# Attention and phase-mixing MLP on one core: theta weights in two loads, and the q/k preparation of two pairs moved to the boundary before theta

## The chip, the core and the metric

The kernel runs on one core of a Trainium2 chip. A core has five engines with a queue of instructions each: TensorE (PE, matrix products and transposes), VectorE (DVE), ScalarE (ACT, table functions and copies), GpSimd (POOL) and SyncE (SP). Each works through its own queue in order and waits on semaphores that the others, or a finished transfer, count up. Transfers between memory and the core run on 16 DMA engines; here POOL issues all loads but two, and SP issues the stores of the output and the transposing transfers.

The metric is the device time of one execution in microseconds (us). The kernel before has a median of 172.26 us in three runs (171.69 to 172.28).

## The reference

```python
# attention, for 4 batches, 8 heads, 768 positions, head size 64
scores = q @ k.T / sqrt(64) - slope[h] * dist        # per head
keep   = (first 8 positions) | (0 <= i - j < 96)
a      = softmax(where(keep, scores, -1e9));  x = a @ v     # x: (4, 768, 512)
# phase-mixing MLP
theta = x @ w_theta                                  # 512 x 512
y = w_tok_r @ (x * cos(theta)) + w_tok_i @ (x * sin(theta)) # 768 x 768 each
u = x + y
out = u + relu(u @ w_ch)                             # 512 x 512
```

Only a band of the scores counts: for each block of 128 keys the queries of the same and of the next block, and the first 8 positions for everybody.

## The kernel before, in words

Heads go in four pairs of two (128 rows for two heads of 64); positions go in six blocks of 128. The stages of a batch, with the names of the functions and the lines of the profile:

- *Loads.* `load_w` (L160) issues on POOL's queue the token weights in six pieces, the theta weights in one transfer of 512 KB (L168), q and k of batch 1, and the channel weights; behind it come v of batch 1 and q and k of batch 2. All these loads convert float32 to bfloat16 on the way. v of batch 2 and the first half of the heads of q and k of batch 3 are issued during batch 0's mixing. `load_behind` (L496) lets POOL copy one element of xT of batch 1 (the "gate", L497) and issues the other half of batch 3's q and k, and its v, behind that copy. The queue's transfers take turns on eight completion semaphores, so each waits until the eighth transfer before it has landed.
- *Preparation of q and k, `prep`* (L249) for one batch and pair: DVE copies q and k of the pair into `qkn` (L246, two copies a pair, for two pairs at once at the start), PE transposes six blocks each of q and k (L261), DVE brings q's transposes to `qT` (L265) and ACT k's to `kT` (L267), and DVE makes `kG` from `kT` (L235, L237). Batch 3's q and k are transposed by SP's transfers instead (`prep_dma`).
- *Scores and values.* `score_mms` (L319) fills a bank group `pb`; there are two such groups, and values use them too. ACT takes the exponential (L329), DVE multiplies by a table of the bias (L338, L341). `values` (L381) multiplies by v and by `vG` (v with the global rows, DVE L359, L360); DVE divides by the row sums into `x_sb` (L386, L388).
- *xT.* `xtrans` turns `x_sb` of a pair into `xT`. For pairs 0, 1 and 2 of batches 1 and 2 it is a transposing transfer on SP's queue (L392); for pair 3 it is six PE transposes (L399) and an ACT copy (L400).
- *Theta.* `theta` (L422) multiplies `xT` by the theta weights, four blocks of 128 inner elements for each of the six position blocks, in the order block 0, 1, 2 (3 last) so that pair 2's `xT` is first needed by the third product. ACT takes cosine and sine (L432), DVE multiplies them with x into `zri` (L436).
- *Mixing.* `mix` (L447) multiplies the transposed token weights with `zri`, DVE adds x into `u` (L452). `utrans` turns `u` (PE L465 and an ACT copy L466, or an SP transfer L461). `chan` (L475) multiplies by the channel weights, DVE adds relu and `u` (L480), SP stores the result (L482).

While batch b is mixed, the attention of batch b+1 runs: `weave` puts the steps of both into one order by weights given by hand. Before the change, the preparation of pairs 0 and 1 of batch 2 is a part of that weave for b = 0 (list `ahead`, L652), that of pairs 2 and 3 is in the weave for b = 1. At the boundary between two batches stands a list `order` (L654): the first remaining `chan` group of batch b-1, four pieces of theta of batch b, another `chan` step, the rest of theta, the rest of `chan`.

Up to `manual.close()` (L642) each engine's order is as written. Behind it a scheduler sets each engine's order from the order of issue and from what each instruction needs, so the position of an instruction on its engine is read from the built program. `behind(...)` keeps a preparation's instructions behind the last one named there on the same engine.

Of the kernel before, what the change touches and what calls it, by code (L numbers as in the profile page):

```python
# [16 lines left out]
def kernel(  # L17
# [13 lines left out]
    nc = tc.nc  # L31
    B, H, S, D = q.shape
    T = 128
    NT = S // T
    DM = H * D
    NC = DM // T
    NP = H // 2
# [18 lines left out]
    def ps_small(shape, dtype):  # L56
        return small.tile(shape, dtype, name="ps", tag="ps")
# [5 lines left out]
    def alloc_qk(b):  # L63
        loads[b] = [ld.tile([T, 2, H, NT, D], BF, name="qk"), None]

    def alloc_v(b):
        vn = loads[b][1] = ld.tile([T, H, NT, D + 1], BF, name="vn")
        nc.vector.memset(vn[:, :, :, D:D + 1], 1.0)

    def load_qk(b, h0, n, which=(0, 1)):  # L70
        qk = loads[b][0]
        for i_ in which:
            nc.gpsimd.dma_start(
                out=qk[:, i_, h0:h0 + n].rearrange("p h t d -> p h (t d)"),
                in_=(q, k)[i_][b, h0:h0 + n].rearrange("h (p t) d -> p h (t d)", p=T))
# [10 lines left out]
    def load_v(b, h0, n):  # L86
        vn = loads[b][1]
        nc.gpsimd.dma_start(out=vn[:, h0:h0 + n, :, 0:D].rearrange("p h t d -> p (h t) d"),  # L88
                            in_=v[b, h0:h0 + n].rearrange("h (t p) d -> p (h t) d", p=T))
# [8 lines left out]
    for i_, eng in ((1, nc.sync), (0, nc.scalar)):  # L98
        eng.dma_start(out=qk32[:, i_].rearrange("p h t d -> p h (t d)"),
                      in_=(q, k)[i_][0, 0:2].rearrange("h (p t) d -> p h (t d)", p=T))  # L100
# [54 lines left out]
    w_theta_bf = const.tile([T, NC, DM], BF)  # L155
# [2 lines left out]
    w_tokT = [const.tile([T, NT, S], BF, name=f"w_tokT_{wi}") for wi in range(2)]  # L158

    def load_w():  # L160
        for tt in range(0, NT, 2):
            for wi, src in enumerate((moe_w_tok_r, moe_w_tok_i)):
                w2 = moe.tile([T, 2, S], BF, name="w_nat", bufs=6)
                nc.gpsimd.dma_start(
                    out=w2, in_=src[tt * T:(tt + 2) * T, :].rearrange("(a p) s -> p a s", p=T))
                w_nat[wi, tt], w_nat[wi, tt + 1] = w2[:, 0], w2[:, 1]
            if tt == 0:
                nc.gpsimd.dma_start(out=w_theta_bf, in_=moe_w_theta.rearrange("(c p) n -> p c n", p=T))  # L168
            if tt == NT - 4:
                load_all_qk(1)  # L170
        nc.gpsimd.dma_start(out=w_ch_bf, in_=moe_w_ch.rearrange("(c p) n -> p c n", p=T))

    def trans_w(tt, copy=nc.vector.tensor_copy, wide=False, copy0=nc.vector.tensor_copy):
        pb = big.tile([T, 2, 2 * 512], BF, name="pbw", tag="pb") if wide else None
        tiles = [pb[:, wi, 0:S].rearrange("p (t n) -> p t n", t=NT) if wide else ps_small([T, NT, T], BF)
                 for wi in range(2)]
        for wi, ps in enumerate(tiles):
            for st in range(NT):
                nc.tensor.transpose(ps[:, st, :], w_nat[wi, tt][:, st * T:(st + 1) * T], ident)
            if not wide:  # L180
                (copy if wi else copy0)(out=w_tokT[wi][:, :, tt * T:(tt + 1) * T], in_=ps)
        for wi, ps in enumerate(tiles if wide else ()):
            (copy if wi else copy0)(out=w_tokT[wi][:, :, tt * T:(tt + 1) * T], in_=ps)  # L183
# [17 lines left out]
    def behind(eng):  # L201

        return tc.issue_after(anchor[eng]) if eng in anchor else nullcontext()
# [25 lines left out]
    def kglob(b, p, t0=0, t1=NT - 2, copy=nc.vector.tensor_copy):  # L229
        kT = qkT[(b, p)][1]  # L230
        if t0 == 0:
            qkT[(b, p)][2] = att.tile([T, NT - 2, T], BF, name="kG", bufs=6)
        kG = qkT[(b, p)][2][:, t0:t1]
        with behind("zri" if p else "dve") if b == B - 1 else nullcontext():
            copy(  # L235
                out=kG, in_=kT[:, (t0 + 1) * T:(t1 + 1) * T].rearrange("p (t n) -> p t n", t=t1 - t0))
            copy(out=kG[:, :, 0:NG], in_=kT[:, None, 0:NG].to_broadcast([T, t1 - t0, NG]))  # L237
# [3 lines left out]
    def prep_copy(b, p):  # L241
        qk = loads[b][0]
        qkn = qkns[b, p] = att.tile([T, NT, 2, 2, D], BF, name="qkn", bufs=2)
        with behind("dve"):
            for i_ in range(2):
                nc.vector.tensor_copy(  # L246
                    out=qkn[:, :, i_].rearrange("p t h d -> p h t d"), in_=qk[:, i_, 2 * p:2 * p + 2])

    def prep(b, p):  # L249
        if p == 0 or (b, p) == (2, NP // 2):  # L250
            prep_copy(b, p)
        if p + 1 < NP and (b, p) != (2, NP // 2 - 1):
            prep_copy(b, p + 1)
        qkn = qkns[b, p]
        qT = att.tile([T, S], BF, name="qT", bufs=6)
        kT = att.tile([T, S], BF, name="kT", bufs=6)
        for i_, dst in ((0, qT), (1, kT)):
            ps = ps_small([T, NT, T], BF)
            with behind("pe"):
                for t_ in range(NT):  # L260
                    nc.tensor.transpose(ps[:, t_, :], qkn[:, t_, i_].rearrange("p h d -> p (h d)"), ident)  # L261
            dst = dst.rearrange("p (n t) -> p n t", t=NT)
            src = ps.rearrange("p t n -> p n t")
            if i_ == 0:
                nc.vector.tensor_copy(out=dst, in_=src)  # L265
            else:
                nc.scalar.copy(out=dst, in_=src)  # L267

        qkT[(b, p)] = [qT, kT, None]
        kglob(b, p)  # L270

    def prep_dma(b, p):
        qk = loads[b][0]
        qkT[(b, p)] = [None, None, None]
        for i_ in (1, 0):
            to = qkT[(b, p)][i_] = att.tile([T, S], BF, name=("qT", "kT")[i_], bufs=6)
            with behind("sp"):
                nc.sync.dma_start_transpose(
                    out=to.rearrange("p (t s) -> p t s", t=NT),
                    in_=qk[:, i_, 2 * p:2 * p + 2].rearrange("p h t d -> p (h t d)"))  # L280
# [204 lines left out]
    def load_all_qk(b):  # L485
        alloc_qk(b)
        load_qk(b, 0, 8)

    def load_all_v(b):
        alloc_v(b)  # L490
        load_v(b, 0, 8)
# [39 lines left out]
    def weave(main, side, s0=0.0, s1=1.0):  # L531
# [11 lines left out]
        while i_ < len(side):  # L543
            side[i_][1]()
            i_ += 1

    load_w()
    load_all_v(1)
    load_all_qk(2)
    alloc_x(0)  # L550
    dve, act = nc.vector.tensor_copy, nc.scalar.copy
    warm(6)
# [53 lines left out]
    p = NP - 1  # L606
# [39 lines left out]
    rest = []  # L646
    for b in range(B):
        nxt = b + 1 if b + 1 < B else None
        lag = 3
        th = [lambda c=c, j=j: theta(b, c, j) for c in range(NT // 2) for j in range(2)]  # L650
        pre = [lambda p=p: prep(1, p) for p in range(NP)] if b == 0 else []
        ahead = [[lambda p=p: prep(2, p) for p in range(NP // 2)], [lambda p=p: prep_dma(3, p) for p in range(1)],  # L652
                 [], []][b]
        order = rest[:1] + th[:4] + rest[1:2] + th[4:] + rest[2:] if b else []  # L654
        if b == 2:
            order[:0] = [lambda p=p: prep_dma(3, p) for p in range(1, NP)]
        if b == 1:
            order.insert(0, lambda: load_behind(3, xT_sb[1][0:1, NC - 1, 0:1]))
        for f in order:
            f()  # L660
        main = []
        for tt in range(0 if b else 2, NT):
            for g in range(NT // 2):
                if (b, tt) != (B - 1, NT - 1):
                    main.append((2048, lambda tt=tt, g=g: mix(b, tt, g)))
                if b == 0 and g == 1 and 4 <= tt + 2 < NT:
                    main.append((1536, lambda tt=tt: trans_w(tt + 2)))
                if tt >= lag and g == 0 and (b, tt) != (B - 1, NT - 1):
                    main.append((2048, lambda tt=tt: chan(b, tt - lag)))
                if b == 0 and g == 1:  # L670
                    main.append((512, lambda tt=tt: utrans(b, tt - 1)))
                if (b, tt, g) == (0, 2, 0):
                    main.append((512, lambda: utrans(0, 0)))
            if b and (b, tt) != (B - 1, NT - 1):
                main.append((0, lambda tt=tt: utrans(b, tt)))
        side = [(1536, f) for f in pre]
        if b == 0:
            side[:0] = [(0, lambda: load_all_v(2))]
            side.append((0, lambda: (alloc_qk(3), load_qk_tokens(3, 0, H // 2))))
        side += attention_steps(nxt, ahead) if nxt else []  # L680
        weave(main, side, 0.1 if b == 0 else 0.0, 0.9)
        rest = [lambda tt=tt, b=b: chan(b, tt) for tt in range(NT - lag, NT)]
        if b == 0:
            rest.insert(1, lambda b=b: utrans(b, NT - 1))
# [44 lines left out]
```

## Time and profile before

| What | us |
|---|---|
| median of three runs | 172.26 |
| span of the profiled execution (first to last instruction) | 170.0 |
| median less that span (start and end around it) | 2.3 |
| PE busy / DVE busy / ACT busy / POOL busy | 158.1 / 125.9 / 102.1 / 37.6 |
| theta weights: issued, landed | 9.98, 24.48 |
| v of batch 2: issued, landed | 39.86, 62.4 |
| first product of theta of batch 0 / third of batch 1 | 24.56 / 70.73 |

Of the profiled execution only the span is given, not a time of its own; the third line is therefore a difference between two executions. The granted clock of PE is 1.00 in all stretches. PE's busy share is high all through (its matmuls are pipelined and a group's busy time overlaps the next), so the page's busy row says little; what counts is which engine a stretch waits for. The chain of work that ended last gives that, the timeline of each engine gives the order of the instructions and their idle times, and the transfers' view gives the time from issue to landing.

### The profile page before, as it was taken

What the parts mean: (1) busy time and instruction counts of PE and PEld (TensorE: products, weight loads), DVE (VectorE), ACT (ScalarE), POOL (GpSimd) and SP (SyncE); (2) the same over time, 40 slices, a digit from 0 to 9 for tenths busy, and PEclk for the clock granted to TensorE, in tenths of its full rate; (3) what the DMA queues carried; (4) which work ended last, traced back from release to release, by engine and by line L of the source; (5) the groups of instructions that cost most, each with busy time, mean ns of one, the idle gap of its engine ahead of it and who ended that gap; (6) DMA issues with size and microseconds to landing.
All of it is one profiled execution on the core that took longest, in us unless ns stands there. A gap on an engine that the chain in (4) does not pass through costs nothing.

```text
span 170.0 us, 3773 instructions
## 1 busy us (share of the span) xinstructions
PE 158.1 (93%) x1544; PEld 85.4 (50%) x1566; DVE 125.9 (74%) x267; ACT 102.1 (60%) x131; POOL 37.6 (22%) x45
## 2 busy tenths in 40 slices
PE   7679999999989899799999999999999999999991
PEld 2346765657645555345555464444554644444440
DVE  6748877699989999957998787788776847614432
ACT  4698898995596585399954561899257309400010
POOL 8976319005262110696000000000000000000000
PEclk9999999999999999999999999999999999999999
DMA  4999999999999999999996879688135472233335
GB/s 147 205 171 179 210 207 205 203 209 180 152 203 189 188 153 182 127 163 149 184 112 57 165 167 130 132 152 241 35 77 139 113 169 80 109 61 93 93 93 185
DMA packets 73488, 25.53 MB, mean 150 GB/s; under 512 B 61568, under 2 KB 70528, under 8 KB 73472
## 3 DMA queue, kind: packets, MB, share of 16 engines
q0 software_dynamic: 45680, 12.45, 77.1%
q1 hardware_dynamic: 27376, 12.33, 32.9%
q10 hardware_dynamic: 416, 0.52, 0.9%
q8 instruction: 12, 0.20, 0.5%
q14 instruction: 4, 0.03, 0.0%
HBM read 25.69 MB, written 6.29 MB: 188 GB/s over the span
## 4 chain that ended last, share of the span: by engine, by line
PE 56%; DMA 19%; DVE 16%; ACT 6%; issue 2%; DVEq 0%
PE ps L447 26%; DMA vn<-in_v_dram 14%; PE ps L475 9%; PE pb L422 6%; PE pb L319 4%; PE pb L381 3%; PE ps L422 3%; DMA xT<-x_sb 3%; DMA qk<-in_k_dram 3%; DVE x_sb L388 3%; DVE e L338 2%; ACT e L329 2%; PE ps L215 1%; ACT cs L432 1%; DVE e L341 1%
## 5 line engine op out<-in xcount | busy, mean ns | idle before, releaser
L447 PE MATMUL ps<-zri,w_tokT 128*128 128x512 bf16 x272 | 67.5, 380 | 1.1 <-issue 0.3
L329 ACT ACTIVATE e<-pb 128x1024 bf16<-128x1024 f32 (+1 forms) x48 | 43.4, 954 | 17.4 <-PE pb L319 17.0
L447 PEld LDWEIGHTS <-w_tokT 128*128 128x128 bf16 x288 | 25.9, 98 | 27.8 <-DVE w_tokT L183 0.6
L452 DVE TENSOR_TENSOR u<-x_sb,ps 128x512 bf16<-128x512 bf16 x24 | 16.3, 680 | 11.7 <-PE ps L447 11.6
L475 PE MATMUL ps<-w_ch_bf,uT 128*128 128x512 bf16 (+1 forms) x96 | 24.1, 371 | 0.2
L436 DVE TENSOR_TENSOR zri<-x_sb,cs 128x1024 bf16<-128x1024 bf16 (+1 forms) x30 | 16.6, 581 | 6.3 <-ACT cs L432 6.1
L480 DVE SCALAR_TENSOR_TENSOR o_sb<-ps,u 128x512 f32<-128x512 f32 (+1 forms) x25 | 16.4, 663 | 4.1 <-PE ps L475 4.1
L319 PE MATMUL pb<-qT,kT 64*128 64x128 bf16 x224 | 15.4, 219 | 2.2 <-DVE qT L226 1.2
L338 DVE TENSOR_TENSOR e<-e,etab 128x1024 bf16<-128x1024 bf16 (+1 forms) x24 | 14.8, 618 | 3.1 <-ACT e L329 3.0
L432 ACT ACTIVATE cs<-pb,halfpi 128x1024 bf16<-128x1024 f32 x8 | 8.9, 1116 | 12.5 <-PE pb L422 12.4
L422 PE MATMUL pb<-w_theta_bf,xT 128*128 128x512 bf16 x62 | 15.0, 379 | 1.1 <-DMA xT<-x_sb 0.9
L319 PEld LDWEIGHTS <-kT 64*128 64x128 bf16 x224 | 8.9, 94 | 13.2 <-issue 11.3
L466 ACT COPY uT<-ps 128x512 bf16<-128x512 bf16 x7 | 4.2, 594 | 18.3 <-PE ps L465 18.1
L381 PEld LDWEIGHTS <-e 128*128 128x128 bf16 x352 | 13.0, 97 | 4.3 <-issue 1.6
L422 PEld LDWEIGHTS <-xT 128*128 128x128 bf16 x96 | 9.1, 98 | 11.8 <-DMA xT<-x_sb 1.9
L475 PEld LDWEIGHTS <-uT 128*128 128x128 bf16 x100 | 9.1, 98 | 9.6 <-ACT uT L466 0.8
L88 POOL DMA_DIRECT2D vn<-in_v_dram x5 | 9.6, 1915 | 12.7 <-DVE qkn L246 10.4
L319 PE MATMUL pb<-qT,kG 64*128 64x128 bf16 x128 | 11.5, 216 | 0.3 <-DVE kG L237 0.2
L388 DVE TENSOR_TENSOR x_sb<-pb,rec 128x768 bf16<-128x768 f32 x12 | 11.4, 953 | 0.3
L381 PE MATMUL pb<-vn,e 128*128 128x65 bf16 x168 | 9.9, 193 | 0.7 <-DVE x_sb L388 0.3
L341 DVE TENSOR_TENSOR e<-e,etab 128x1024 bf16<-128x1024 bf16 x12 | 8.2, 687 | 2.4 <-ACT e L329 2.4
L267 ACT COPY kT<-ps 128x768 bf16<-128x768 bf16 x8 | 6.4, 798 | 4.6 <-PE ps L261 4.4
(81 smaller groups left out, 209.4 us busy)
## 6 DMA issues: line engine op xcount, KB each, us to landing
out_dram<-o_sb SPq DMA_DIRECT2D x23, 256.0 KB, 2.3
vn<-in_v_dram POOLq DMA_DIRECT2D x3, 768.0 KB, 22.5
qk<-in_q_dram POOLq DMA_DIRECT2D x2, 768.0 KB, 21.1
qk<-in_k_dram POOLq DMA_DIRECT2D x2, 768.0 KB, 24.2
w_nat<-in_moe_w_tok_r_dram POOLq DMA_DIRECT2D x3, 384.0 KB, 15.7
w_nat<-in_moe_w_tok_i_dram POOLq DMA_DIRECT2D x3, 384.0 KB, 15.2
vn<-in_v_dram POOLq DMA_DIRECT2D x2, 384.0 KB, 10.2
qk<-in_q_dram POOLq DMA_DIRECT2D x8, 96.0 KB, 8.6
```

The source lines that it names most:

```text
L319: nc.tensor.matmul(pb[:, hh, o:o + T], lhsT=lhsT, rhs=qT[R, (own, nxt)[part]], start=bool(b), stop=bool(b) or (jt == NT - 1 or (j == 1 and ...
L329: ins = nc.scalar.activation(e_c, pb[:, :, 0:n], AF.Exp, scale=scale).ins
L338: nc.vector.tensor_mul(e_c, e_c, tab[:, :, s0:s0 + n // T].rearrange("p a s n -> p a (s n)"))
L381: nc.tensor.matmul(po4[:, head - h0, it - i0], lhsT=l_, rhs=r_, start=(i_ == 0), stop=(i_ == len(mms) - 1))
L388: nc.vector.tensor_mul(xv, po4[:, :, :, 0:D], rec.to_broadcast([T, n, nt, D]))
L422: nc.tensor.matmul(pb[j_] if last else pb[:, j_, :], lhsT=xT[:, dc, st(j_)], rhs=w_theta_bf[:, dc, :], start=(dc == 0), stop=(dc == NC - 1))
L432: nc.scalar.activation(o, p_, AF.Sin, **bias)
L436: anchor["zri"] = nc.vector.tensor_mul(zri[b][:, i_, 2 * c + j_:2 * c + j_ + n, :].rearrange("p j (g d) -> p j g d", g=NP), xb[:, :, 2 * c ...
L447: anchor["pe"] = nc.tensor.matmul(ps, lhsT=w_tokT[wi][:, st, tt * T:(tt + 1) * T], rhs=zri[b][:, wi, st, :], start=(st == 0 and wi == 0), ...
L452: anchor["dve"] = nc.vector.tensor_add(u_sb[b, tt].rearrange("p (g d) -> p g d", g=NP), x_sb[b][:, :, tt, :], ps.rearrange("p (g d) -> p g ...
L475: nc.tensor.matmul(ps_c, lhsT=uT[:, dc, :], rhs=w_ch_bf[:, dc, i_ * n:(i_ + 1) * n], start=(dc == 0), stop=(dc == NC - 1))
L480: nc.vector.scalar_tensor_tensor(o_sb[:, cols], in0=ps_c, scalar=0.0, in1=u[:, cols], op0=ALU.max, op1=ALU.add)
```

## The change

Two things change. In `load_w`, the theta weights come in two transfers of 256 KB, blocks 0 and 1 and then blocks 2 and 3; the order of everything else on POOL's queue is the same, now written out. And the preparation of pairs 0 and 1 of batch 2 is taken out of the weave of batch 0 with the attention of batch 1 and put into the list `order` at the boundary of batch 1, behind the first remaining `chan` group of batch 0 and ahead of theta of batch 1.

```diff
     def load_w():
-        for tt in range(0, NT, 2):
-            for wi, src in enumerate((moe_w_tok_r, moe_w_tok_i)):
+        def tok(tt, wis=(0, 1)):
+            for wi, src in [(w_, (moe_w_tok_r, moe_w_tok_i)[w_]) for w_ in wis]:
                 w2 = moe.tile([T, 2, S], BF, name="w_nat", bufs=6)
...
-            if tt == 0:
-                nc.gpsimd.dma_start(out=w_theta_bf, in_=moe_w_theta.rearrange("(c p) n -> p c n", p=T))
-            if tt == NT - 4:
-                load_all_qk(1)
+        def wth(lo, hi):
+            nc.gpsimd.dma_start(out=w_theta_bf[:, lo:hi], in_=moe_w_theta.rearrange("(c p) n -> p c n", p=T)[:, lo:hi])
+        tok(0)
+        wth(0, 2)
+        wth(2, 4)
+        tok(2)
+        load_all_qk(1)
+        tok(4)
         nc.gpsimd.dma_start(out=w_ch_bf, in_=moe_w_ch.rearrange("(c p) n -> p c n", p=T))
+        load_all_v(1)
+        load_all_qk(2)
...
     load_w()
-    load_all_v(1)
-    load_all_qk(2)
...
-        ahead = [[lambda p=p: prep(2, p) for p in range(NP // 2)], [lambda p=p: prep_dma(3, p) for p in range(1)],
+        ahead = [[], [lambda p=p: prep_dma(3, p) for p in range(1)],
                  [], []][b]
-        order = rest[:1] + th[:4] + rest[1:2] + th[4:] + rest[2:] if b else []
+        pr = [lambda p=p: prep(2, p) for p in range(NP // 2)]
+        order = rest[:1] + pr + th[:4] + rest[1:2] + th[4:] + rest[2:] if b == 1 else rest[:1] + th[:4] + rest[1:2] + th[4:] + rest[2:] if b else []
```

In the built program the number of instructions is the same on every engine but POOL, which has one more transfer. SP's order is unchanged. On PE, the 24 transposes of the two preparations stand directly before theta of batch 1, whose first two products no longer stand before the transposes of x_sb of pair 3. On DVE and ACT the scheduler also places some steps of the weave differently: DVE's copies to `vG` of batch 1 stand behind the first two and three products of batch 1's table multiplication, not before them.

## The prediction

> **What bounds the kernel now.** I read the page's chain of work that ended last first. By line it is TensorE (PE) almost throughout, but its timed form shows two stretches where it leaves PE: 48.6 to 70.7 us, while attention of batch 1 is woven into the mixing of batch 0, and 4.6 us ahead of 115.7, where batch 2's scores wait for ACT. The first is where this change works (times from the span's start, then length):
>
> ```profile
> 48.60 0.71 DVE vG L359
> ...
> 61.38 0.87 DVE qT L265
> 62.25 0.20 DVE kG L235
> ...
> 64.50 0.81 DVE qT L265
> 65.31 0.86 DVE x_sb L388
> 66.17 0.03 DVE kG L235
> 66.20 4.49 DMA xT<-x_sb
> 70.69 0.05 issue
> 70.73 0.39 PE pb L422
> 71.12 0.05 issue
> 71.17 2.75 PE pb L422 x12
> ```
>
> The reader is to see VectorE (DVE) following itself without a gap, then 4.5 us of one transposing transfer, then theta of batch 1 on PE. The windows view says how full the engines are there and later (length, then busy us of PE, its weight loads, DVE, ACT, POOL):
>
> ```profile
> 47.50:66.00 18.50, 16.77 (x235) 10.39 (x238) 17.76 (x38) 14.16 (x18) 4.95 (x6) 1.00 1.94 184
> 66.00:70.73 4.73, 3.77 (x24) 1.63 (x23) 4.70 (x12) 1.29 (x2) 1.08 (x2) 1.00 1.72 172
> 78.00:88.00 10.00, 9.79 (x107) 5.56 (x108) 8.82 (x17) 8.97 (x11) 1.04 (x1) 1.00 1.73 155
> 88.00:98.00 10.00, 9.89 (x114) 5.17 (x113) 7.63 (x13) 4.57 (x5) 0.00 (x0) 1.00 0.70 107
> ```
>
> Up to 70.7 DVE is the full engine and PE loses time; from 78 on PE has hardly a gap, so what is won or lost before 70.7 should reach the end one for one. Last, the transfers of SP's queue, by issue windows (median us to landing), for xT of pairs 0, 1 and 2, the store between the first two, and a kT, qT pair in a quiet time:
>
> ```profile
> xT<-x_sb SPq DMA_TRANSPOSE x1, 7.6
> ...
> out_dram<-o_sb SPq DMA_DIRECT2D x1, 256.0 KB, 6.9
> ...
> xT<-x_sb SPq DMA_TRANSPOSE x1, 8.4
> ...
> xT<-x_sb SPq DMA_TRANSPOSE x1, 4.5
> ...
> kT<-qk SPq DMA_TRANSPOSE x1, 2.8
> qT<-qk SPq DMA_TRANSPOSE x1, 2.8
> ```
>
> Issued at 56.60, 57.96, 59.54 and 66.20, the first four land at 64.2, 64.9, 67.9 and 70.7: in order, and slowly while POOL's load of v of batch 2 (issued 39.86, 22.5 us to landing, 62.4) fills the engines. These transfers decide my number.
>
> **The change, part by part.** *The theta split.* One more issue on POOL, about 0.75 us by the 0.80 us of the 512 KB one. POOL's transfers rotate over eight completion semaphores, so the seven behind the split each wait for one transfer later than before: the k load of batch 1, issued at 14.86, now waits for the v load that lands at 19.05. None of it moves a landing as long as the queue stays full: it lands in order of issue (w_nat 20.17 and 21.97, theta 24.48, w_nat 26.4), and at 19 us five loads are still ahead. From the v load of batch 1 on (25.43) the waits are the same transfers again. The gain is bounded too: theta's first product starts at 24.56, 0.08 behind the landing, and the next steps wait for DVE's x_sb. I take 0; ends -0.1 and, if the queue ran dry for the extra issue, +0.75. The Trainium skill, page "DMA: Bandwidth & Descriptors", section "Anatomy of one DMA", speaks against the split: about 2.0 us fixed for each such transfer. Here 384, 512 and 384 KB land 1.80, 2.51 and 1.96 us apart, in proportion to size, so in a full queue that constant is not seen; by the rule v of batch 1 would land at 50.6 instead of 48.6 and stall DVE by about 1 us.
>
> *Prep of two pairs leaves the weave.* Out of DVE go four qkn copies (chain: 0.21+0.54+0.27 = 1.02), two qT evacuations (0.87+0.81), and two kG pairs (0.20+0.41 and 0.20+0.08): 3.6 us. Out of PE go 24 transposes, 1.34 (L261 x12 is 0.67); out of ACT two kT copies of 0.80, which has idle time. No DMA is issued by the step, and SP's order is the same.
>
> How much earlier does x_sb of pair 3 end, which before is at 68.1? By DVE: the changed order issues from the first table product on, which can start at 48.5, twelve e products (6.7), the two vG copies (1.3), two w_tokT (0.93), two u (1.1), two o_sb (1.2) and four rec and x_sb (4.0): 15.3, so 63.8. Walking that list against ACT's exponentials (0.95, 0.95 and 0.72 a pair from 47.0) adds about 0.9: the score banks are two and the scores of pairs 2 and 3 wait for x_sb of pairs 0 and 1. By PE: 68.1 less its waits in the stretch (0.41+0.19+0.22+0.27+0.16+0.17+0.17 = 1.6), less 1.34, less the two theta products that stood before it (0.43), gives 64.7. I take 64.7, 3.4 earlier; if PE keeps its waits it is 66.3. The vG copy also moves behind two products, so DVE's 0.73 wait for v of batch 1 has work in front of it.
>
> *The same prep in front of theta.* From 64.7, PE does the transposes of x_sb (0.35), waits for u (0.6) and turns it (0.25), does one chan group (0.86), the 24 transposes (1.34) and two theta products (0.43): the third theta product, the first to need pair 2's xT, can start at 68.5, against 70.73 before: 2.2 earlier, not 3.4. The transposes wait for the qkn copies (u 0.6, then 1.05, ready at 66.4), and behind them on PE is theta, for which ACT and DVE wait. Their cover is the chan group, done at 66.7; if the copies came as late as 67.8, the third product could start at 69.6, still not past the 69.7 found below. On ACT the kT copies end near 69.0, before the cosine. On DVE the prep fills the 1.30 us idle before zri (73.39) and ends near 71.3, before the cosine (about 72.1); if it came 2 us later, PE reaches the mix that needs zri only some 5 us after that.
>
> *What is late next.* Pair 2's xT is issued when its x_sb ends: about 63.1 instead of 66.2. But SP's transfers land in order, and pair 0's, issued 1 us earlier, still meets the v load until 62.4. So I leave pair 1's landing at 67.9. Behind it pair 2's takes between 1.3 (kT to qT in the quiet time: issued at 96.87 and 98.20, 2.8 each) and 3.0 (pair 1 behind the store): 69.2 to 70.9. In the trace's packet records pair 1 moves from 64.5 to 66.9; a transfer already queued would move for the same 2.3 from there and land 0.5 later, 69.7. I take that, nearer the short end because its descriptors wait ready. The third theta product goes from 70.73 to about 69.75: **1.0 us won**. Against it works a thing that the change triggers: POOL's gate copy waits for ACT's xT (69.59), which is now ready at about 66.1, so the second half of batch 3's q and k joins the engines 3.5 us sooner, while that xT moves. The end 70.9 is for that. Other end: the transfer is not held at all and lands 4.5 after issue, 67.6; then PE's 68.5 counts.
>
> The same page, section "Queues, rings and completion order", says that an engine alternates between queues packet by packet, which speaks for that other end: SP's transfers would not sit behind a whole POOL load. The 7.6 and 8.4 us against 2.8 do not look so; by the rule the sum would be -2.2, by the rows -1.0.
>
> *Sum.* Span 170.0 - 1.0 = 169.0. The median of the three runs, 172.26, is 2.3 above the profiled span, which I take as what lies around it: **171.3 us**. Half a per cent, 0.86 us, is about what a measurement of this kernel tells from no change.
>
> **The rivals.** *Held by PE alone.* Pair 0's and 1's transfers also start sooner, pair 2's lands before 68.5, and all 2.2 arrive: 170.0. For it: the issues are 1 to 3 us earlier. Against: the 7.6 and 8.4 us rows.
>
> *It does not do what it says.* The last xT lands where it did, because the v load's end and the sooner gate hold it: PE finishes early and waits longer for theta. Third product 70.5 to 70.9, 172.1 to 172.4. For: the trace shows pair 2's packets slow at 68 to 69.5 beside POOL's. Against: its descriptors are now queued early.
>
> *Slower.* The weave does not shorten, and the prep is only put in front of theta. Its place is the wait of scores of pairs 2 and 3 for x_sb of pairs 0 and 1, through the two score banks: if that keeps the old pace (x_sb of pair 3 at 68.1), the path from there to the third theta product is 3.8 instead of 2.6 us, +1.2: 173.5. It decides as soon as x_sb of pair 3 gains less than 1.2 us. Against: DVE, full from 48.6 on, loses 3.6 us of work.
>
> **How the numbers follow.** The forecast (xT lands at 69.2 to 70.1) 0.45, held by PE 0.17, no effect 0.20, slower 0.18. The forecast's own range is 170.7 to 171.7. Over all, 169.8 to 172.9 leaves out the rest of the slower case and some of the best. Faster by over 0.5%: 0.36 of the forecast and 0.17, 0.53. Within: 0.09 and 0.20, 0.29. Slower: 0.18.
>
> **What would show it.** Right: in the profile after, x_sb of pair 3 ends near 64.7; PE runs the 24 prep transposes right before theta, then waits 1 to 1.5 us for DMA xT; theta's third product near 69.7; the mixes of batches 1 to 3 unchanged in length. The prediction is wrong if theta starts without a wait (held by PE), if the wait grows to 2 us or more (no effect), if x_sb of pair 3 ends after 66.9 (slower), or if v of batch 1 lands clearly after 48.6 (the split costs).

## The result, and the profile after

The changed kernel takes 173.89 us (median of six runs, 173.31 to 175.34), the kernel before on the same chip 171.92 (171.69 to 172.28): 1.0128 times as long, interval 1.0094 to 1.0163. It is slower, and above the upper end of the range. The span of the profiled execution is 171.9 us (forecast 169.0, before 170.0); that execution's own time is 173.81, so 1.9 us lie around the span, not the 2.3 that the prediction took. All six executions have a mean granted clock of PE of 0.977 to 0.990; 0.990 is what 3.41 us at half clock make of this span.

The timed form of the chain of waits of the changed kernel, around the boundary ahead of theta of batch 1 (start, length, what):

```profile
61.54 0.56 DVE e L344
62.10 0.15 DVE rec L392
...
62.27 0.96 DVE x_sb L394
...
63.26 7.59 DMA xT<-x_sb
...
70.90 2.53 PE pb L428 x6
...
73.45 1.12 ACT cs L438
...
74.60 0.69 DVE zri L442
```

VectorE's run of work ends 2.9 us sooner than before, and pair 2's transfer starts at 63.26, as forecast (63.1). But it now takes 7.59 us where it took 4.49, and PE starts the third theta product at 70.90, not at 69.75; before it was 70.73, as the timeline of PE of the kernel before has it:

```profile
70.73 3.19 PE L422 MATMUL pb<-w_theta_bf,xT 128*128 128x512 bf16 x13 [0.90 <-DMA xT<-x_sb]
```

The transfers' view gives the three xT of batch 1 in the changed kernel, issued at 55.73, 58.40 and 63.26 (last number: us to landing):

```profile
xT<-x_sb SPq DMA_TRANSPOSE x1, 7.7
...
xT<-x_sb SPq DMA_TRANSPOSE x1, 9.5
...
xT<-x_sb SPq DMA_TRANSPOSE x1, 7.6
```

They land at 63.4, 67.9 and 70.9; before, at 64.2, 67.9 and 70.7. The last two have not moved, though they were issued 1.1 and 2.9 us earlier. The timeline of PE in the changed kernel (start, length, instructions; in brackets the idle time before and what ended it):

```profile
66.46 1.50 PE L267 MATMUL ps<-ident,qkn 128*128 128x128 bf16 x24
67.80 0.59 PE L428 MATMUL pb<-w_theta_bf,xT 128*128 128x512 bf16 x2
70.90 4.88 PE L428 MATMUL pb<-w_theta_bf,xT 128*128 128x512 bf16 x14 [2.50 <-DMA xT<-x_sb]
```

PE is done with its own work at 68.4 (forecast 68.5) and then stands for 2.5 us, against 0.9 before. And the 14 theta products behind the wait take 4.88 us. Why, the windows view shows (length, then busy us of PE, its weight loads, DVE, ACT and POOL, then the granted clock of PE, DMA share and GB/s):

```profile
68.00:69.00 1.00, 0.40 (x2) 0.07 (x1) 1.00 (x3) 0.83 (x2) 1.00 (x2) 1.00 1.43 137
69.00:70.00 1.00, 0.00 (x0) 0.00 (x0) 1.00 (x4) 0.00 (x0) 1.00 (x2) 1.00 2.47 162
...
71.00:72.00 1.00, 1.00 (x4) 0.33 (x4) 0.73 (x2) 0.00 (x0) 1.00 (x1) 0.58 1.60 268
72.00:73.00 1.00, 1.00 (x4) 0.39 (x3) 0.00 (x0) 0.00 (x0) 1.00 (x3) 0.50 2.23 176
73.00:74.00 1.00, 1.00 (x3) 0.30 (x2) 0.00 (x0) 0.55 (x1) 0.79 (x1) 0.50 2.42 154
74.00:75.00 1.00, 1.00 (x5) 0.43 (x4) 0.40 (x1) 1.00 (x2) 0.84 (x1) 0.71 2.41 153
```

The granted clock is the third number from the right: 1.00 until 0.27 us behind the idle time, then 0.5 from 71.17 to 74.58, 3.41 us in all, then 1.00 again. In the profile before it is 1.00 in every stretch. The same 14 products take 3.19 us at full clock (the run with filled idle time, below), so the half clock costs 4.88 - 3.19 = 1.7 us. With the third product 0.17 us later that makes 1.9, which is the whole difference of the spans (171.9 - 170.0): what is lost here reaches the end one for one.

### The profile page after: what moved, and what is told of

It is laid out like the page before. It is cut to its first block, busy times and chain, and to the rows that moved or that the text cites. A ratio compares the mean times of both kernels' runs of the same rounds, so it can differ in the third digit from the quotient of the medians.

```text
span 171.9 us, 3796 instructions
## 1 busy us (share of the span) xinstructions
PE 160.3 (93%) x1566; PEld 85.2 (50%) x1566; DVE 127.2 (74%) x267; ACT 102.3 (60%) x131; POOL 38.9 (23%) x46
## 4 chain that ended last, share of the span: by engine, by line
PE 65%; DVE 17%; ACT 8%; DMA 7%; issue 1%; DVEq 0%; ACTq 0%
PE ps L453 31%; PE ps L481 8%; PE pb L428 7%; PE pb L325 5%; DMA xT<-x_sb 4%; ACT e L335 4%; PE pb L387 4%; PE ps L428 3%; DMA qk<-in_k_dram 2%; DVE qT L271 2%; ACT cs L438 2%; DVE x_sb L394 2%; DVE qkn L252 2%; DVE e L344 2%; PE ps L405 1%; DVE zri L442 1%
## 5 line engine op out<-in xcount | busy, mean ns | idle before, releaser
L453 PE MATMUL ps<-zri,w_tokT 128*128 128x512 bf16 x288 | 70.3, 380 | 0.1
L428 PE MATMUL pb<-w_theta_bf,xT 128*128 128x512 bf16 x64 | 16.6, 411 | 2.5 <-DMA xT<-x_sb 2.5
L82 POOL DMA_DIRECT2D qk<-in_q_dram x8 | 7.0, 871 | 9.1 <-DVE qkn L252 3.8
```

Source lines behind the costliest of these rows:

```text
L428: nc.tensor.matmul(pb[j_] if last else pb[:, j_, :], lhsT=xT[:, dc, st(j_)], rhs=w_theta_bf[:, dc, :], start=(dc == 0), stop=(dc == NC - 1))
L453: anchor["pe"] = nc.tensor.matmul(ps, lhsT=w_tokT[wi][:, st, tt * T:(tt + 1) * T], rhs=zri[b][:, wi, st, :], start=(st == 0 and wi == 0), ...
```

## The experiments

Two questions were tested: whether the split of the theta load or the move is the cause, and within the move, what makes xT of pair 2 late and what the half clock costs. In the expectations theory W is the account with the late transfer and the half clock behind the wait, from the tokens-late run on with POOL's loads as what holds the transfer; the other letters are its rivals. Ratios are to the kernel before, run on the same chip. An edit is shown against the changed kernel where it is not said otherwise.

**The split alone.** The kernel before, with only the theta weights in two loads; the edit takes the move out of the changed kernel:

```diff
-        ahead = [[], [lambda p=p: prep_dma(3, p) for p in range(1)],
+        ahead = [[lambda p=p: prep(2, p) for p in range(NP // 2)], [lambda p=p: prep_dma(3, p) for p in range(1)],
...
-        order = rest[:1] + pr + th[:4] + rest[1:2] + th[4:] + rest[2:] if b == 1 else rest[:1] + th[:4] + rest[1:2] + th[4:] + rest[2:] if b else []
+        order = rest[:1] + th[:4] + rest[1:2] + th[4:] + rest[2:] if b == 1 else rest[:1] + th[:4] + rest[1:2] + th[4:] + rest[2:] if b else []
```

> The kernel before with the split of the theta weights alone; the preparation stays in the weave. Theory W (theta of batch 1 waits for the transposing transfer of xT of pair 2, and TensorE's clock is halved behind that wait; the split has no part in it): as before, within 0.3 us, granted clock 1.00 throughout. Rival S (the extra transfer, which delays the k load of batch 1 and what waits behind it, costs the time): 1 to 2 us slower than before.

Measured: 172.0 us, 0.9985 (0.9959 to 1.0012). The timeline of PE of this kernel, at the third theta product:

```profile
70.63 3.20 PE L428 MATMUL pb<-w_theta_bf,xT 128*128 128x512 bf16 x13 [1.17 <-DMA xT<-x_sb]
```

The split costs nothing that can be measured. An idle time of 1.17 us is followed by products at full clock.

**The move alone.** The changed kernel with the theta weights in one transfer:

```diff
-        wth(0, 2)
-        wth(2, 4)
+        wth(0, 4)
```

> The changed kernel with the theta weights in one transfer again; the move of the preparation alone. Theory W: as the changed kernel within 0.3 us (about 2 us slower than before), TensorE idle for about 2.5 us ahead of the third theta product of batch 1, clock halved for some 3.4 us behind it. Rival S: as before.

Measured: 174.42 us, 1.0111 (1.0073 to 1.015). The timeline of PE of this kernel:

```profile
71.25 4.88 PE L427 MATMUL pb<-w_theta_bf,xT 128*128 128x512 bf16 x14 [1.98 <-DMA xT<-x_sb]
```

The move makes the whole loss. Here 1.98 us of idle time were enough for the half clock, again 3.41 us long (71.55 to 74.97).

**Idle time filled.** The changed kernel with 12 products on zeros, which nobody reads, between the second and the third theta product; `held` is the theta product before, so that the order of theta and fill is kept:

```diff
+            if (b, c, j, dc) == (1, 0, 0, 1):
+                fill = ps_small([T, 512], FP)
+                for _ in range(12):
+                    with tc.issue_after(held):
+                        held = nc.tensor.matmul(fill, lhsT=zero[:, 0:T], rhs=zero, start=True, stop=True).ins
```

> The changed kernel with 12 products on zeros (2.6 us of TensorE at full clock) between the second and the third theta product of batch 1, where TensorE waits for the transfer. They compute nothing that is used. Theory W: the transfer lands as in the changed kernel, 70.9 into the span, the clock stays at 1.00, and the time falls by 1.7 us (half of 3.4 us) to about 0.2 us above before. Rival P (the 24 transposes and their copies ahead of theta are themselves what costs): no gain, as the changed kernel or up to 0.3 us slower.

Measured: 172.6 us, 1.0021 (0.9999 to 1.0043); span 170.6. The timeline of PE of this kernel:

```profile
68.02 2.75 PE L436 MATMUL ps<-zero 128*128 128x512 bf16 x12
71.33 3.19 PE L430 MATMUL pb<-w_theta_bf,xT 128*128 128x512 bf16 x14 [0.55 <-DMA xT<-x_sb]
```

xT lands no sooner than in the changed kernel (71.28 against 70.85), PE starts theta even 0.4 us later, and the kernel is 1.3 us faster: in this profile the clock stays at 1.00 all through and the 14 products take 3.19 us. So the half clock is most of the loss, and what is left is the late xT.

**The gate later.** The changed kernel with POOL's gate on the first product for `zri` in place of the xT of pair 3:

```diff
-            order.insert(0, lambda: load_behind(3, xT_sb[1][0:1, NC - 1, 0:1]))
+            order.insert(len(pr) + 4, lambda: load_behind(3, zri[1][0:1, 0, 0, 0:1]))
```

> The changed kernel with the gate of POOL's last loads of batch 3 tied to the first zri product of batch 1 instead of the xT copy, so these loads start behind theta (near 75 us instead of 66.7). Theory W in the form that pair 2's transfer can start only when pair 1's has landed, and is then slow beside the loads issued earlier: it lands at 70.5 to 70.9 as in the changed kernel, and the time is within 0.4 us of it. Rival G (the earlier gate puts loads beside that transfer and holds it): it lands at 69 to 69.7, the wait falls to some 1 us, the clock stays at 1.00, and the time is 1.0 to 2.5 us below the changed kernel.

Measured: 175.02 us (173.78 to 177.06 in four executions), 1.0191 (1.0117 to 1.0265), 1.1 us above the changed kernel and not within 0.4 of it; the time alone is too scattered to say more. The loads behind the gate start at 75.25 and not at 66.7, and xT of pair 2 lands at 70.72, 0.13 earlier than in the changed kernel; PE waits 2.4 us and then has 3.41 us of half clock. Theory G falls: the earlier gate does not hold that transfer. Nor does it start only when pair 1's has landed, as theory W has it here: in the packet records its packets begin at 66.84, and pair 1's lands at 67.88.

**Batch 3's tokens late.** The changed kernel with all of batch 3's q and k behind the gate, so that POOL's queue has no load of them before 67:

```diff
-            side.append((0, lambda: (alloc_qk(3), load_qk_tokens(3, 0, H // 2))))
+            side.append((0, lambda: alloc_qk(3)))
...
-            load_qk_tokens(b, H // 2, H // 2)
+            load_qk_tokens(b, 0, H)
```

> The changed kernel with all eight heads of batch 3's q and k issued behind the gate, so that POOL's queue carries nothing between the end of the v load of batch 2 (62.4) and the gate (66.7). Theory W, with POOL's loads holding SP's transposing transfers: pair 2's xT, issued at 63.3, lands at 66.5 to 68.5, TensorE hardly waits, the third theta product comes at 68.3 to 68.6, the clock stays at 1.00, and the time is 2.0 to 2.4 us below before (near 169.8). Rival Q (SP's queue is slow by itself in that stretch, whatever POOL does): it lands near 70.8 again and the time stays near that of the changed kernel.

Measured: 171.43 us, 0.9937 (0.9904 to 0.997). The transfers' view of this kernel for xT of pair 2, issued at 63.73, and the timeline of PE:

```profile
xT<-x_sb SPq DMA_TRANSPOSE x1, 2.7
```

```profile
66.93 1.50 PE L267 MATMUL ps<-ident,qkn 128*128 128x128 bf16 x24
68.49 3.40 PE L428 MATMUL pb<-w_theta_bf,xT 128*128 128x512 bf16 x15
71.72 0.39 PE L471 MATMUL ps<-ident,u 128*128 128x128 bf16 x4
```

Theory W stands: without those loads beside it the transfer takes 2.7 us, the quiet time's price, lands at 66.5, and theta runs through without a wait and at full clock. The row shows 15 of the 16 products; by what PE does next, the transposes of u (71.72, before 73.76), theta ends 2.0 us sooner than before. The span falls by 0.5 only, and the time misses the expected 169.8. The windows and the waits of this kernel show where the rest goes:

```profile
75.00:78.00 3.00, 2.29 (x24) 1.05 (x23) 3.00 (x6) 2.98 (x5) 3.00 (x4) 1.00 1.57 115
...
88.00:98.00 10.00, 9.30 (x104) 4.68 (x105) 7.53 (x12) 5.07 (x6) 0.00 (x0) 1.00 2.59 153
```

```profile
PE ps L453 <- DVE o_sb L486: 0.6, 1, 0.6
...
PE ps L481 <- DMA uT<-u: 0.4, 1, 0.4
```

At 75 to 78 PE loses 0.71 us (before: none), and DVE, for whose `o_sb` it waits, is busy in all three of them. At 88 to 98 PE loses 0.70 (before 0.11, about what matmul records missing from that trace make): 0.4 waiting for the transposing transfer of `u`, which is issued at 86.70 and lands at 95.20, beside loads of POOL that now run until 95.2, and 0.26 waiting for DVE's `x_sb`. 2.0 - 0.71 - (0.70 - 0.11) is 0.7; the 0.2 us between that and the span's 0.5 is not placed.

**The same on the kernel before**, as a control; the edit is the same.

> The same on the kernel before: the control. Theory W: pair 2's xT is issued at 66.2 and lands near 69.0 to 69.5 instead of 70.7; TensorE is busy until 69.8, so the third theta product moves from 70.7 to about 69.9: 0.5 to 0.9 us faster than before. Rival Q: as before.

Measured: 171.59 us, 0.995 (0.9914 to 0.9986). xT of pair 2, issued at 66.06, lands at 68.81, also 2.7 us, and the third product starts 1.2 us sooner than before (69.55 against 70.73):

```profile
69.55 3.19 PE L422 MATMUL pb<-w_theta_bf,xT 128*128 128x512 bf16 x13
```

The windows of this kernel at 88 to 98, and its longest wait of PE:

```profile
88.00:98.00 10.00, 8.57 (x93) 4.27 (x94) 6.90 (x11) 4.22 (x5) 0.00 (x0) 1.00 2.16 151
```

```profile
PE ps L475 <- DMA uT<-u: 1.4, 1, 1.4
```

PE loses 1.43 us there (before 0.11). In this execution (172.26 us, span 170.3) that undoes the whole gain of the first boundary, where the delayed loads now lie; over ten executions some of it is left. The loads beside SP's transfers, not the order of the preparation, set the landing in both orders.

**xT of pair 2 by PE.** The changed kernel, and as a control the kernel before, with pair 2's x_sb of batch 1 transposed by PE and copied by ACT:

```diff
-        if b > 2 or (b and p < NP - 1):
+        if b > 2 or (b and p < NP - 1 - (b == 1)):
```

> The changed kernel with xT of pair 2 of batch 1 made by six transposes on TensorE and an ACT copy instead of SP's transfer. Theory W: the wait that is left is for pair 1's xT (66.3 to 67.9); behind it stand 18 transposes of the preparation (1.0 us) and 15 theta products, done near 72.1 against 73.7 in the kernel before; the clock stays at 1.00; 1.4 to 1.8 us faster than before. Rival P (the preparation ahead of theta costs by itself): no faster than before.

> The same on the kernel before, the control. x_sb of pair 3 still ends near 68 there, since VectorE is full; the 0.9 us wait at the third theta product goes, six transposes (0.35 us) come: 0.3 to 0.8 us faster than before. If it gained as much as the run with the changed kernel, the move would have no part in the gain.

Measured: 172.36 us, 1.002 (0.9989 to 1.005), for the changed order, and 171.96, 1.0002 (0.996 to 1.0044), for the old. The first misses its forecast gain of 1.4 to 1.8 us; for the second no gain is measured, though the interval still holds the lower half of its 0.3 to 0.8. In the changed order the wait for pair 2's transfer is gone as expected and theta's products end at 72.4 at full clock. The windows of that kernel, and its wait:

```profile
72.00:75.00 3.00, 3.00 (x18) 1.40 (x16) 3.00 (x8) 3.00 (x4) 3.00 (x3) 1.00 2.30 146
75.00:78.00 3.00, 2.02 (x10) 0.79 (x9) 3.00 (x7) 2.98 (x6) 0.65 (x1) 1.00 1.18 75
```

```profile
PE ps L453 <- DVE o_sb L486: 0.9, 1, 0.9
```

PE loses 0.98 us at 75 to 78, while DVE is busy in every one of the six microseconds. DVE's timeline in this kernel says with what:

```profile
68.82 1.80 DVE L271 COPY qT<-ps 128x768 bf16<-128x768 bf16 x2
70.54 0.78 DVE L241 COPY kG<-kT 128x512 bf16<-128x512 bf16 x2
...
72.51 0.67 DVE L442 TENSOR_TENSOR zri<-x_sb,cs 128x1024 bf16<-128x1024 bf16 x1
...
73.73 1.27 DVE L442 TENSOR_TENSOR zri<-x_sb,cs 128x1024 bf16<-128x1024 bf16 x2
74.93 0.88 DVE L252 COPY qkn<-qk 128x768 bf16<-128x768 bf16 x1
...
76.59 0.68 DVE L486 SCALAR_TENSOR_TENSOR o_sb<-ps,u 128x512 f32<-128x512 f32 x1
```

None of these has an idle time in front. As soon as theta is on time, the moved preparation (3.6 us of DVE) and the next `qkn` copies stand ahead of and among `zri` and `o_sb`, and DVE is late next. In the control DVE has idle time there (2.31 us busy of 3 at 72 to 75, 2.43 at 75 to 78), and its times lie apart: seven from 171.4 to 172.2 with a mean granted clock of 0.987 to 1.00, three from 173.6 to 173.9 with 0.97. The kernel before has such executions too on that chip (five at 0.97, 172.83 to 173.04 us). Without those at 0.97 on either side the medians are 171.62 and 171.99, 0.4 us of gain; this choice was made after the result was known and shows only that the forecast gain is not ruled out.

**Only pair 0 ahead of theta.** The kernel with the tokens late, with pair 1's preparation behind theta; the edit of the tokens is as above:

```diff
-        order = rest[:1] + pr + th[:4] + rest[1:2] + th[4:] + rest[2:] if b == 1 else rest[:1] + th[:4] + rest[1:2] + th[4:] + rest[2:] if b else []
+        order = rest[:1] + pr[:1] + th[:4] + rest[1:2] + th[4:] + pr[1:] + rest[2:] if b == 1 else rest[:1] + th[:4] + rest[1:2] + th[4:] + rest[2:] if b else []
```

> Batch 3's tokens all behind the gate, as in the kernel with the tokens late, and of the moved preparation only pair 0 ahead of theta of batch 1; pair 1's stands behind theta. Theory D (VectorE gives the gain back: the moved copies stand in front of and among the zri products, so PE waits for o_sb at 75 to 78): about 1.9 us of copies (qT 0.94, kG 0.44, half of the qkn copies 0.55) and 12 transposes of PE (0.67) leave the path ahead of theta; theta's 16 products end about 0.6 earlier than with the tokens late, PE's idle time at 75 to 78 (0.29 + 0.42) shrinks to under 0.3, and the time falls by 0.3 to 0.9 us against the kernel with the tokens late (171.43), that is 170.5 to 171.1, ratio to before 0.988 to 0.992. Theory R (the gap only moves: pair 1's preparation is then late for the scores of batch 2, or uT late at 88 to 98): 171.2 to 171.9.

Measured: 170.26 us (169.78 to 170.55), 0.988 (0.9856 to 0.9905). The timeline of PE of this kernel, and its windows:

```profile
67.63 3.62 PE L428 MATMUL pb<-w_theta_bf,xT 128*128 128x512 bf16 x16
...
78.61 0.83 PE L267 MATMUL ps<-ident,qkn 128*128 128x128 bf16 x12
```

```profile
72.00:75.00 3.00, 2.69 (x34) 1.73 (x33) 2.62 (x4) 3.00 (x6) 3.00 (x5) 1.00 1.52 97
75.00:78.00 3.00, 2.85 (x14) 1.31 (x14) 3.00 (x8) 2.98 (x5) 3.00 (x4) 1.00 1.81 119
78.00:88.00 10.00, 10.00 (x108) 5.57 (x108) 8.76 (x18) 7.00 (x9) 5.78 (x6) 1.00 2.30 174
88.00:98.00 10.00, 10.00 (x120) 5.40 (x120) 7.86 (x14) 5.92 (x7) 0.00 (x0) 1.00 2.22 163
```

This kernel beats both the kernel before and the changed one, and its ratio is the one that theory D gave, but the gain is not where D put it. The wait for `o_sb` is gone and the loss at 75 to 78 shrinks from 0.71 to 0.15 us, as D said; at 72 to 75, however, PE now loses 0.31 (with all of the preparation ahead of theta: none). The next transposes of `qkn`, pair 2's of batch 2, start at 78.61, and in the kernel with the tokens late at this one:

```profile
78.65 0.83 PE L267 MATMUL ps<-ident,qkn 128*128 128x128 bf16 x12
```

Up to there the order has won next to nothing. What it wins, 0.9 us of span (169.5 to 168.6), comes mostly from 88 to 98, where PE's 0.70 us of idle time are gone. Neither theory foresaw that, and why it closes was not tried.

**Less fill.** The filled kernel with `range(4)` in place of `range(12)`, to find how much idle time halves the clock.

> The changed kernel with 4 instead of 12 products on zeros between the second and third theta product: they end about 69.3, and PE is then idle for about 1.6 us until xT of pair 2 lands at 70.9. Theory C1 (an idle time between 1.2 and 1.6 us or less is short enough to keep the clock): clock 1.00, theta's 14 products take 3.19 us, time about 172.6 as with 12. Theory C2 (1.6 us already halves the clock): 14 products take 4.88 us after a wait, 3.41 us at clock 0.5, time 173.8 to 174.4.

Measured: 172.7 us (171.68 to 174.73), 1.0031 (1.0001 to 1.006). It does not tell C1 from C2. In the profiled execution the clock was at 0.5 in a stretch between 8 and 18 us, the boundary came some 2.8 us later than in the changed kernel, and xT was there before the fill ended (timeline of PE):

```profile
71.03 1.03 PE L436 MATMUL ps<-zero 128*128 128x512 bf16 x4
71.89 3.18 PE L430 MATMUL pb<-w_theta_bf,xT 128*128 128x512 bf16 x14
```

No idle time was left to judge in that profile.

## Why the prediction was wrong

**Right.** *The split at 0*: 0.9985; v of batch 1 lands at 48.59 in the changed kernel, 48.58 before. *The weave shortens*: x_sb of pair 3 ends at 65.0 (forecast 64.7, from 68.1), so the rival "Slower" did not happen, though its sign came true, for another reason. *PE's path*: 68.4 against 68.5, with the transposes at 66.46, right when the qkn copies were to be ready. *The issue of pair 2's xT*: 63.26 against 63.1.

**Wrong in size: "I take that", 69.7 for the landing of pair 2's xT.** It landed at 70.85, the upper end of the 69.2 to 70.9 given. The step looked at the load of v of batch 2, which ended at 62.4, and had the queued transfer start at 66.9, move for 2.3 us like pair 1's and land 0.5 later. In the packet records of the changed kernel it starts at 66.99, moves for 2.98 us and lands 0.88 later, which is the 1.15 us. Its start agrees by luck: pair 1's packets, which it was to follow, now end at 65.84. What held it were the other loads of POOL's queue, the first half of batch 3's q and k, of which the last are issued at 56.46 and 63.26: with these away it takes 2.7 us, in the changed order and in the old one. The gate, named as the reason for the upper end, was not it, so that end met the landing by luck. So of the rivals the first half of "It does not do what it says" came true: the transfer landed where it did, and the wait grew past the 2 us that the prediction set as the mark. This is 1.15 us of the 2.9 by which the span missed.

**Missing: the clock.** This is the larger part of the miss. Every term of the sum had PE at 1.00, as in all rows of before, and none was set down for a clock that falls behind a wait. That rival priced a longer wait at nothing beyond the lateness (172.1 to 172.4) and so ended at "no change". A PE that is done with its work 1.4 us earlier (68.4 and not 69.8) and waits for the same landing is not in the same state: 2.5 us idle, then 3.41 us at half rate, 1.7 us lost. With this term the rival's price would have been its 172.1 to 172.4 plus 1.7, that is 173.8 to 174.1, or 173.4 to 173.7 with the 1.9 us measured around the span; 173.89 was measured. The Trainium skill, page "TensorE: Matmul & The Clock Gate", section "HAM oscillation — how this bites in real kernels", tells of matrix work that waits for a transfer and then runs at half clock, and gives about 3.4 us of idle time as the mark. The half rate agrees with the rows here (0.50); the mark does not, as 1.98 and 2.50 us of idle time were enough.

**Hidden by the two.** "What is won before 70.7 should reach the end one for one" was not tried by the changed kernel, which won nothing; its loss did reach the end one for one. In the runs that did win there it held only in part: 0.5 of 2.0 us with the tokens late. The prediction's cover for DVE's part (the prep done at 71.3, before the cosine) is right only as long as theta is as late as forecast; the earlier it starts, the more of the 3.6 us stands in front of `zri`.

**Open.** Why SP's transposing transfers are held beside POOL's loads was not tried; only that they are. What mark of idle time, or of work in a stretch, halves the clock is narrowed below but was not set by a run of its own. Where in the kernel the executions with a mean clock of 0.97 run at half clock is not recorded. Why the gap at 88 to 98 closes in the fastest kernel was not tried.

## What to carry to other kernels

Work taken off a stretch pays only up to the transfer that the stretch ends with: before moving compute, look at what else the DMA engines carry from that transfer's issue to its landing, and take the quiet row's duration only where it is quiet. If TensorE will get to a wait earlier without the wait ending earlier, price the wait twice, once as idle time and once as the half-clock stretch that may follow it; filling it with idle products saved the second here, and putting other real work there was not tried. When the first limit falls, look for the next ones before counting the gain: of the 2.0 us won at the boundary with the tokens late, later waits took most, and with half of the preparation behind theta the kernel gained more, but not at the place for which that was done.

## What was not expected of the hardware

- A TensorE idle time of 1.98 to 2.50 us was followed by 3.41 us at half the granted clock (three kernels, the same length each time: 71.17 to 74.58, 71.55 to 74.97, 71.24 to 74.66); after 0.9 and 1.17 us it was not.
- The clock records of all twelve traces lie on a grid: every stretch of full or half clock that begins and ends inside the record is a whole multiple of 3.413 us (in the changed kernel 64.85 at full clock, 19 of them, then one at half; with less fill 10.24 at half, three of them). The grid stretch just ahead of the three drops above held 0.91, 1.38 and 0.99 us of PE work; the emptiest at this boundary after which the clock stayed held 2.47 (before), 2.18 (split alone) and 2.86 us (filled). So by these traces it is not an idle time's length alone that counts, but how little work one grid stretch holds. Up to 160 us the clock fell after 0.91 to 1.50 us and stayed after 1.62 or more; at the very end of three kernels it also stayed after 1.43 to 1.55. This is read from twelve traces; no run shifted the grid to test it.
- The transposing transfer of pair 2's xT took 2.7 us with no load of POOL beside it (three kernels) and 4.5 to 8.2 us beside POOL's loads (seven); issued 2.9 us earlier it landed no sooner. In the kernel before, transposing transfers behind POOL's last load took 2.4 to 4.7 us, so its loads are not all that lengthens one.
- Some executions have a half-clock stretch near the start as well (8.43 to 11.85 in the kernel with the tokens late); in the four profiles with one, the grid stretch ahead of it held 1.33 to 1.50 us of PE work. The profiles of the kernels before and after have none (2.11 us or more), and the kernel with pair 1 behind theta has one and is still the fastest. The grid lies differently in each trace (its first recorded stretch begins at 3.83 to 6.95). Executions of one kernel differ too: of 31 of the kernel before on one chip, 17 have a mean granted clock of 1.00 and five of 0.97. That the grid makes this difference fits, but is not shown, as there is one trace of each kernel.
